# Turned probabilities of the first and the third unit in the places of two late weight blocks, with the order laid out anew, in a block-sparse attention kernel with a channel mixer

## The chip, the cores and the metric

The kernel runs on one core of a Trainium2 chip. The metric is the device time of one launch in microseconds (us), the median over runs. Nothing is shared with other cores. The program is one straight line of instructions for each engine: TensorE (PE, with its weight loads PEld), VectorE (DVE), ScalarE (ACT), GpSimd (POOL), and SyncE (SP), which issues all transfers.

## The reference

Attention with a block mask over 4 batches, 8 heads, 768 tokens and 64 channels, then a gated mixer over the 512 joined channels:

```python
scores = scale * np.matmul(q, k.transpose(0, 1, 3, 2))
mask = np.abs(blk_i - blk_j) <= window
mask = mask | (blk_i == 0) | (blk_j == 0) | (blk_i == n_blocks - 1) | (blk_j == n_blocks - 1)
for qb in range(n_blocks):
    for kb in sampled_blocks[qb]:
        mask[qb * block:(qb + 1) * block, kb * block:(kb + 1) * block] = True
...
attn = attn / (np.sum(attn, axis=-1, keepdims=True) + 1e-09)
attn_out = np.matmul(attn, v).astype(np.float32)
x = np.ascontiguousarray(attn_out.transpose(0, 2, 1, 3)).reshape(B, S, H * D)
...
xk = mu_k * x + (1.0 - mu_k) * x_prev;  xr = mu_r * x + (1.0 - mu_r) * x_prev
k = np.maximum(xk @ w_k, 0.0)
v = k * k @ w_v
r = 1.0 / (1.0 + np.exp(-(xr @ w_r)))
return (r * v).astype(np.float32)
```

A block is 32 tokens, so there are 24 blocks. Three blocks per query block are drawn at random and known only at run time. The three weight matrices arrive with 8 bytes for an element.

## The kernel before

**Units.** The attention is cut into 26 units. Unit u0 holds query block 1 of all four batches, u1 holds block 2, and so on to u21. The last four units are the "wide" ones, with the first and the last block of one batch each. A near unit does, for each half `gi` of the heads: scores on PE into PSUM (tile `s`, L402), the row maximum on DVE (`nm`, L412), four exponentials on ACT (`p`, L423), the probabilities turned, and the product with the values on PE (tile `o`, L436 or L475). Units u0 to u3 turn their probabilities with PE transposes (tile `t`, L371), two groups of four for each half, and each group is then copied from PSUM into the tile `pt` by ACT (L375) or DVE (L376). From u4 on the turning is a DVE transpose and a move by transfers. After the products DVE divides by the row sum (`x`, L556 to L567), and PE turns the result for the mixer (`tx`, L597).

**Loads of a unit.** The keys of a near unit stand in eight of the twelve slots of `KA`, its values in `VA`: the two edge blocks, the three near blocks (a ring of three slots, so that a unit loads one new near block), and the three drawn ones, whose numbers SP reads from the tile `packed`. A new near block goes into the slot whose block the unit before was the last to read, so SP waits for PE before it issues that load: L284 for keys, L297 for values. SP issues everything in order, so whatever is queued behind such a load waits too. The program rotates eight transfer semaphores, so a transfer is issued once the one eight places before it has landed.

**Weights.** 20 blocks w0 to w19 of 128 x 512 are loaded with 8 bytes for an element (L187; w0 to w3 of `w_r`, w4 to w11 of `w_k`, w12 to w19 of `w_v`), and each is brought into a high and a low part by six steps that go to ACT, DVE or POOL (size, tail, sign, join, hi, lo). Each block has a place of its own in the on-chip memory, with its own tag.

**Mixer.** Twelve tiles of 256 tokens: gates `r`, hidden units `h`, values `v`, each product as three terms of high and low parts. The first tile needs units u0 to u3.

**What sets the order.** Every step is recorded in a plan. The list `ORDER` says in which order the steps are written out, for all engines together, and `CHOICE` says which engine takes a step that has several ways. Each engine runs its own steps in that order. The tile `pt` has one buffer: `PT_BUFS` is 1, so the first copy into a unit's `pt` waits until the products of the unit before have read theirs.

Of the kernel before, what the change touches and what calls it, by code (L numbers as in the profile page):

```python
# [19 lines left out]
P = 128  # L20
# [10 lines left out]
QB = 4  # L31
# [64 lines left out]
def block_sparse_attention_channel_mix(  # L96
# [262 lines left out]
    def turned(name):  # L359

        return buf([P, 2, 8, P], F32, "pt", PT_BUFS, f"pt{name}")

    def turn(parts, pt, gi, k, name):
# [5 lines left out]
        def tr():  # L369
# [5 lines left out]
            (ACT, 464, 0, lambda: nc.scalar.copy(pt.ap[:, gi, to], tp.ap[:, 0:many])),  # L375
            (DVE, 600, 0, lambda: nc.vector.tensor_copy(out=pt.ap[:, gi, to], in_=tp.ap[:, 0:many])),  # L376
        ], reads=[(tp,)], writes=[(pt, (gi, k))])
# [5 lines left out]
    def near_unit(at, q, first, o):  # L383
# [6 lines left out]
        for gi in range(2):  # L390
# [39 lines left out]
            def pv(pt=pt, gi=gi):  # L430
                for row in range(2):
                    for a in range(2):
                        i, h = 2 * a + row, 4 * gi + 2 * a + row
                        for g in range(2):
                            for j in range(QB):
                                nc.tensor.matmul(  # L436
                                    o[gi].ap[ROWS[j], i * DV : (i + 1) * DV], pt.ap[:, gi, 4 * row + 2 * a + g, ROWS[j]],
                                    VA.ap[:, c0 + g, j, h * DV : (h + 1) * DV], start=(g == 0), stop=(g == 1), skip_group_check=True)

            plan.add(f"u{name} values", PE, N_PV, pv, reads=[(pt, (gi, 0), (gi, 1))] + [(VA, *PLACE(c0, *range(QB)), *PLACE(c0 + 1, *range(QB)))],  # L440
# [392 lines left out]
X_FROM = 6  # L833
MOVE_FROM = 4
# [160 lines left out]
```

## Time and profile before

| | us |
|---|---|
| median of 3 runs | 515.41 (510.9, 515.41, 519.99) |
| the profiled execution, device time | 516.33 |
| its span (first to last instruction) | 514.6 |
| PE busy | 480.9 (93% of the span) |
| DVE busy | 320.7 (62%) |
| ACT busy | 306.4 (60%) |
| POOL busy | 207.5 (40%) |

A time of the profile is counted from the start of the span. The time around the span is 516.33 - 514.6 = 1.7 us. The profiled execution is 0.9 us above the median. A busy share is an average over the whole program; the stretches differ much, so each stretch is read by itself.

### The profile page before, as it was taken

The numbers are of one execution on the slowest core, as the hardware profiler recorded it, in microseconds if no ns is written. First come the engines' busy times: TensorE is split into PE (matmuls) and PEld (weight loads), VectorE is DVE, ScalarE is ACT, GpSimd is POOL, SyncE is SP. The second block draws the span as 40 slices with busy tenths as digits, with TensorE's granted clock in tenths as the row PEclk, the third lists the DMA queues.
The fourth block names the chain that finished last, engine by engine and source line by source line (L and its number), as shares of the span: only waits on it lengthen the run. The fifth ranks groups of instructions, "written<-read, shape, count | busy, mean of one in ns | idle before, by whom it ended". The sixth has DMA issues, their size and how long they took to land.

```text
span 514.6 us, 18098 instructions
## 1 busy us (share of the span) xinstructions
PE 480.9 (93%) x7384; PEld 399.9 (78%) x7384; DVE 320.7 (62%) x608; ACT 306.4 (60%) x701; POOL 207.5 (40%) x253
## 2 busy tenths in 40 slices
PE   4567899999999998999999999999999999999997
PEld 4254577788788787878778878878778879889896
DVE  3667989786786765775675766664765653334231
ACT  2887988867745646546665846655546574455341
POOL 2435546352610723244442432234543525434531
PEclk9689999999999999999999999999999999999999
DMA  7999999798878889888898888999669653100101
GB/s 265 368 343 379 350 337 310 245 279 249 266 214 252 228 217 270 225 258 236 256 264 240 222 258 265 289 275 340 186 158 309 162 137 85 29 22 20 42 22 41
DMA packets 58052, 114.65 MB, mean 223 GB/s; under 512 B 7665, under 2 KB 20721, under 8 KB 55026
## 3 DMA queue, kind: packets, MB, share of 16 engines
q1 hardware_dynamic: 57970, 113.50, 72.3%
q8 instruction: 58, 0.95, 0.7%
q14 instruction: 24, 0.20, 0.1%
HBM read 77.82 MB, written 6.29 MB: 163 GB/s over the span
## 4 chain that ended last, share of the span: by engine, by line
PE 78%; DMA 8%; SPq 4%; ACT 4%; issue 3%; DVE 2%; POOL 1%; POOLq 0%
PE v L772 22%; PE h_2p L737 7%; PE h_0p L737 6%; PE s L402 6%; PE h_1p L737 6%; PE r_1p L716 6%; PE o L475 6%; PE r_0p L716 6%; PE h_3p L737 6%; DMA VA<-vt 3%; DMA KA<-kt 3%; PE sw L496 2%; PE o L538 2%; ACT p L452 1%; SPq L349 1%
## 5 line engine op out<-in xcount | busy, mean ns | idle before, releaser
L772 PE MATMUL v<-w,k 128*128 128x512 f32 (+1 forms) x600 | 138.9, 385 | 0.0
L772 PEld LDWEIGHTS v<-w,k 128*128 128x128 f32 x600 | 107.9, 188 | 26.7 <-issue 4.6
L402 PE MATMUL s<-KA,q 64*32 64x256 f32 x1408 | 47.6, 391 | 15.7 <-DMA raw<-w_k 10.7
L412 DVE TENSOR_REDUCE nm<-s 128x4 f32<-128x1024 f32 x44 | 53.0, 1215 | 14.3 <-PE s L402 14.0
L452 ACT ACTIVATE p<-s,nm 128x256 f32<-128x256 f32 x144 | 60.6, 479 | 0.6
L455 DVE STREAM_TRANSPOSE r<-p 128x1024 f32<-128x1024 f32 x36 | 43.6, 1229 | 10.9 <-ACT p L452 7.1
L402 PEld LDWEIGHTS s<-KA,q 64*32 64x32 f32 x1408 | 26.2, 109 | 30.2 <-POOL w L246 10.7
L475 PEld LDWEIGHTS o<-VA,pt 128*32 128x32 f32 x2304 | 33.9, 109 | 6.6 <-issue 4.4
L716 PE MATMUL r_0p<-w,xr 128*128 128x512 f32 x144 | 36.8, 400 | 1.3 <-issue 1.3
L475 PE MATMUL o<-VA,pt 128*32 128x65 f32 x2304 | 37.3, 221 | 0.8 <-DMA VA<-vt 0.7
L737 PE MATMUL h_2p<-xk,w 128*128 128x256 f32 x288 | 37.8, 284 | 0.2 <-ACT h_0k L752 0.2
L737 PEld LDWEIGHTS h_0p<-xk,w 128*128 128x128 f32 x288 | 35.6, 189 | 3.0 <-issue 1.6
L737 PE MATMUL h_0p<-xk,w 128*128 128x256 f32 x288 | 37.1, 282 | 0.8 <-issue 0.4
L737 PE MATMUL h_3p<-xk,w 128*128 128x256 f32 x288 | 37.4, 285 | 0.0
L737 PEld LDWEIGHTS h_3p<-xk,w 128*128 128x128 f32 x288 | 35.6, 190 | 2.4 <-issue 1.2
L716 PE MATMUL r_1p<-w,xr 128*128 128x512 f32 x144 | 37.2, 398 | 0.0
L737 PEld LDWEIGHTS h_2p<-xk,w 128*128 128x128 f32 x288 | 35.7, 191 | 1.9 <-issue 0.8
L737 PEld LDWEIGHTS h_1p<-xk,w 128*128 128x128 f32 x288 | 35.3, 189 | 2.3 <-DVE rx L576 1.0
L737 PE MATMUL h_1p<-xk,w 128*128 128x256 f32 x288 | 37.0, 283 | 0.0
L666 ACT ACTIVATE xr_0d<-xt,mk 128x128 f32<-128x128 f32 x48 | 19.3, 403 | 21.9 <-DVE xr_0f L673 15.9
L716 PEld LDWEIGHTS r_0p<-w,xr 128*128 128x128 f32 x144 | 26.2, 188 | 7.7 <-issue 1.8
L716 PEld LDWEIGHTS r_1p<-w,xr 128*128 128x128 f32 x144 | 26.0, 189 | 5.3
(237 smaller groups left out, 818.8 us busy)
## 6 DMA issues: line engine op xcount, KB each, us to landing
VA<-vt SPq DMA_DIRECT2D x92, 260.0 KB, 4.3
KA<-kt SPq DMA_DIRECT2D x89, 256.0 KB, 4.2
pt<-r SPq DMA_DIRECT2D x72, 256.0 KB, 4.9
VA<-vw SPq DMA_DIRECT2D x24, 260.0 KB, 5.5
KA<-kq SPq DMA_DIRECT2D x16, 384.0 KB, 5.0
ptw<-rw SPq DMA_DIRECT2D x32, 192.0 KB, 3.8
out<-z SPq DMA_DIRECT2D x23, 256.0 KB, 3.8
q<-qt SPq DMA_DIRECT2D x22, 256.0 KB, 5.8
```

Source lines behind the costliest of these rows:

```text
L349: nc.sync.dma_start(near_values(chunk, j), vt[bass.ds(sampled_block(n, NRAND + j, nc.sync), 1)].rearrange("o w x -> w (o x)"))
L402: nc.tensor.matmul(s.ap[ROWS[j], row, a * 256 : (a + 1) * 256].rearrange("p (n x) -> p n x", x=BLK), q.ap[half, (hp * QB + j) * BLK : (hp ...
L412: nc.vector.tensor_reduce(out=nm.ap.rearrange("p (r a) -> p r a", r=2), in_=s.ap.rearrange("p r (a x) -> p r a x", a=2), axis=AX.X, op=ALU ...
L452: plan.add(f"u{name} exp {i}", ACT, 365, lambda row=row, a=a, i=i: nc.scalar.activation(squares()[:, :, :, i, :], s.ap[:, row, a * 256 : ( ...
L455: plan.add(f"u{name} turn", DVE, N_TURN, lambda: nc.vector.transpose(out=r.ap[:, :, gi].rearrange("p j c i x -> p j (c i x)"), in_=squares ...
L475: nc.tensor.matmul(o[gi].ap[ROWS[j], i * DV : (i + 1) * DV], pt.ap[:, j, gi, g, 2 * row + a, :], VA.ap[:, c0 + g, j, h * DV : (h + 1) * DV ...
L496: nc.tensor.matmul(s.ap[HALF[a], row, 0:W], q.ap[half, 2 * hp * BLK : 2 * (hp + 1) * BLK], wide_keys(b, hp)[half, k * W : (k + 1) * W], st ...
L538: nc.tensor.matmul(o.ap[ROWS[2 * a + e], c * DV : (c + 1) * DV], pt.ap[:, 2 * a + e, row, n, :], VA.ap[:, c1, part, h * DV : (h + 1) * DV] ...
L666: nc.scalar.activation(parts(d.ap), cols(c, 0), AF.Copy, scale=mk.ap[:, which, c : c + 1])
L716: nc.tensor.matmul(pr.ap[:, 0:512], xr.ap[:, a, c, :], weight_of["r", c].ap[:, w, :], start=(c == 0 and m == 0), stop=(c == CC - 1 and m = ...
L737: nc.tensor.matmul(ph.ap[:, ff * TT : (ff + 1) * TT], weight_of["k", c, f2 // 2].ap[:, w, f % 4 * P : (f % 4 + 1) * P], xk.ap[:, a, c, :], ...
L772: nc.tensor.matmul(pv.ap[:, 0:width], k2.ap[:, a, f, i * P : (i + 1) * P], weight_of["v", f].ap[:, w, cs], start=(f == 0 and m == 0), stop ...
```

## The change

For u0 and u2 the tile of turned probabilities is no longer the one buffer `pt`. Each half goes into the place of a weight block, half 0 into that of w18 and half 1 into that of w19. Those two weight blocks can then be loaded only once u2's products have read their probabilities. u1 and u3 keep the one buffer `pt`. The table `ORDER` is new for the first 584 of its 2139 steps (to about the scores of u8) and the same from there on. Some 80 entries of `CHOICE` differ, all of steps in that first part; the warm-up on PE goes from 128 small matmuls to 1.

```diff
-    def turned(name):
-
-        return buf([P, 2, 8, P], F32, "pt", PT_BUFS, f"pt{name}")
+    def turned(at):
+
+        if at in GUESTS:
+            halves = [buf([P, 8, P], F32, f"w{w}", 1, f"pt{at}_{w}") for w in GUESTS[at]]
+            return halves, lambda gi: halves[gi].ap
+        one = buf([P, 2, 8, P], F32, "pt", PT_BUFS, f"pt{at}")
+        return [one, one], lambda gi: one.ap[:, gi]
...
-            (ACT, 464, 0, lambda: nc.scalar.copy(pt.ap[:, gi, to], tp.ap[:, 0:many])),
-            (DVE, 600, 0, lambda: nc.vector.tensor_copy(out=pt.ap[:, gi, to], in_=tp.ap[:, 0:many])),
-        ], reads=[(tp,)], writes=[(pt, (gi, k))])
+            (ACT, 464, 0, lambda: nc.scalar.copy(pt[1](gi)[:, to], tp.ap[:, 0:many])),
+            (DVE, 600, 0, lambda: nc.vector.tensor_copy(out=pt[1](gi)[:, to], in_=tp.ap[:, 0:many])),
+        ], reads=[(tp,)], writes=[(pt[0][gi], (gi, k))])
...
-                                    o[gi].ap[ROWS[j], i * DV : (i + 1) * DV], pt.ap[:, gi, 4 * row + 2 * a + g, ROWS[j]],
+                                    o[gi].ap[ROWS[j], i * DV : (i + 1) * DV], pt[1](gi)[:, 4 * row + 2 * a + g, ROWS[j]],
...
 X_FROM = 6
+GUESTS = {0: (18, 19), 2: (18, 19)}
 MOVE_FROM = 4
...
 CHOICE = {
-    "warm": 6, "u0 1 1 turned": 1, "u0 put x": 1, "u1 1 0 turned": 1, "u2 0 0 turned": 1, "u3 0 0 turned": 1, "u3 1 0 turned": 1, "u4 put x": 1, "u5 put x": 1, "u6 put x": 1,
+    "warm": 2, "u0 0 1 turned": 1, "u0 1 0 turned": 1, "u0 1 1 turned": 1, "u1 0 0 turned": 1, "u1 0 1 turned": 1, "u1 1 1 turned": 1, "u2 0 1 turned": 1, "u2 1 0 turned": 1,
...
 ORDER = [
-    0, 1, 2, 7, 16, 3, 11, 994, 973, 924, 14, 931, 4, 5, 13, 12, 10, 15, 926, 927, 925, 55, 966, 928, 933, 934, 56, 932, 974, 935, 996, 936, 6, 8, 995, 18, 937, 929, 997, 53,
+    2, 1, 3, 14, 16, 973, 55, 10, 917, 4, 5, 11, 931, 12, 7, 9, 974, 975, 13, 976, 15, 977, 932, 17, 934, 978, 979, 933, 935, 19, 918, 936, 920, 994, 6, 56, 0, 980, 53, 34,
```

**SP, the start of the program.** `raw` is a weight block, `KA` keys, `q` the queries, and the row on `packed` stands right ahead of u0's three drawn key loads. Before:

```order
L159 DMA mk<-mu_r 128x4
L137 DMA drawn<-blocks 1x1848
L284 DMA KA<-kt 128x512
L187 DMA raw_210<-w_k 128x1024
L187 DMA raw_212<-w_k 128x1024
L187 DMA raw_214<-w_r 128x1024
L284 DMA KA<-kt 128x512
L187 DMA raw_217<-w_r 128x1024
L159 DMA mk<-mu_k 128x4
L284 DMA KA<-kt 128x2x512
L305 DMA q_233<-qt 128x512
L266 TENSOR_LOAD packed
```

and with the change:

```order
L137 DMA drawn<-blocks 1x1848
L284 DMA KA<-kt 128x512
L187 DMA raw_78<-w_k 128x1024
L305 DMA q_81<-qt 128x512
L187 DMA raw_83<-w_r 128x1024
L159 DMA mk<-mu_k 128x4
L284 DMA KA<-kt 128x512
L187 DMA raw_98<-w_r 128x1024
L284 DMA KA<-kt 128x2x512
L159 DMA mk<-mu_r 128x4
L266 TENSOR_LOAD packed
```

Three weight blocks instead of four stand ahead of u0's drawn keys, and the drawn block numbers are the first transfer.

**SP, from the load that waits for u0's scores to the last load of u0's values.** `L284 DMA KA` is the near key block of u1, which waits for u0's scores; `L349` are the drawn values of u0, `L297` near or edge values. Before:

```order
L284 DMA KA<-kt 128x512
L187 DMA raw_346<-w_r 128x1024
L187 DMA raw_354<-w_k 128x1024
...
L349 DMA VA<-vt 32x2080
...
L297 DMA VA<-vt 32x2080 x2
L266 TENSOR_LOAD packed
```

and with the change:

```order
L284 DMA KA<-kt 128x512
L187 DMA raw_213<-w_v 128x1024
L297 DMA VA<-vt 32x2080
...
L349 DMA VA<-vt 32x2080
...
L297 DMA VA<-vt 32x2080
L305 DMA q_270<-qt 128x512
L266 TENSOR_LOAD packed
```

Two of u0's near and edge value blocks have gone ahead (they now stand right behind u0's drawn keys), and one weight block instead of two stands between.

**PE, from the end of the warm-up to u0's products.** `s` are scores, `t0` the turns of u0, `o` the products; `pt_371` is the one buffer, `pt_19` and `pt_18` are the new places. Before:

```order
L171 MATMUL warm<-const-bfloat16-1.0 128x64
L402 MATMUL s_1_291<-KA,q_233 32x256 x16
L402 MATMUL s_0_315<-KA,q_233 32x256 x16
...
L371 MATMUL t0 0 0_443<-ident,p_0_362 128x128 x4
L436 MATMUL o_1_472<-VA,pt_371 32x65 x32
L436 MATMUL o_0_511<-VA,pt_371 32x65 x32
L371 MATMUL t1 1 1_557<-ident,p_1_464 128x128 x4
L371 MATMUL t1 1 0_571<-ident,p_1_464 128x128 x4
```

and with the change:

```order
L171 MATMUL warm<-const-bfloat16-1.0 128x64
L406 MATMUL s_1_163<-KA,q_81 32x256 x16
L406 MATMUL s_0_183<-KA,q_81 32x256 x16
...
L375 MATMUL t0 0 0_308<-ident,p_0_224 128x128 x4
L440 MATMUL o_1_328<-VA,pt_19_230 32x65 x32
L440 MATMUL o_0_368<-VA,pt_18_322 32x65 x32
L375 MATMUL t1 1 1_419<-ident,p_1_316 128x128 x4
L375 MATMUL t1 1 0_430<-ident,p_1_316 128x128 x4
```

But for the warm-up the order of PE is the same here: the turns of u1 still stand behind the products of u0. So it is at the two later seams: the turns of u2 stand behind the products of u1, and those of u3 behind the products of u2, before and now.

## Rows read from the trace of the kernel before

**Rows 1.** Page, part 2: busy tenths in 40 slices of 12.9 us.

```profile
PE   4567899999999998999999999999999999999997
```

**Rows 2.** Stretches: PE, PEld, DVE, ACT, POOL busy; granted clock; transfer share; GB/s.

```profile
15.00:30.00 15.00, 8.53 (x144) 4.55 (x144) 11.79 (x16) 12.72 (x28) 6.81 (x6) 0.78 0.98 365
30.00:45.00 15.00, 10.92 (x326) 8.61 (x327) 10.13 (x20) 12.77 (x29) 5.13 (x5) 0.89 0.99 361
45.00:60.00 15.00, 11.56 (x294) 8.24 (x301) 12.23 (x32) 12.36 (x34) 8.57 (x11) 1.00 0.96 357
75.00:90.00 15.00, 14.26 (x266) 12.44 (x265) 14.45 (x28) 12.53 (x27) 8.01 (x9) 1.00 0.94 316
200.00:300.00 100.00, 97.98 (x1584) 82.12 (x1584) 66.55 (x130) 63.55 (x150) 42.34 (x53) 1.00 0.86 247
```

**Rows 3.** Timeline of PE: start, length, tiles, count, idle before and its releaser.

```profile
0.77 5.81 PE L171 MATMUL warm<-const-bfloat16-1.0 128*128 128x64 bf16 x128 [0.77 <-PEq L943]
17.23 3.67 PE L402 MATMUL s<-KA,q 64*32 64x256 f32 x64 [10.65 <-DMA raw<-w_k]
31.89 3.65 PE L436 MATMUL o<-VA,pt 128*32 128x65 f32 x128 [4.06 <-DMA VA<-vt]
46.45 0.43 PE L436 MATMUL o<-VA,pt 128*32 128x65 f32 x14 [2.62 <-issue]
46.81 0.66 PE L371 MATMUL t2 0 0_757<-ident,p 128*128 128x128 f32 x4
57.98 1.09 PE L402 MATMUL s<-KA,q 64*32 64x256 f32 x32
60.62 1.12 PE L436 MATMUL o<-VA,pt 128*32 128x65 f32 x64
66.68 2.67 PE L402 MATMUL s<-KA,q 64*32 64x256 f32 x64 [0.82 <-DMA KA<-kt]
69.28 0.96 PE L716 MATMUL r_0p<-w,xr 128*128 128x512 f32 x3
```

**Rows 4.** Chain that ended last, 25 to 67 us: start, length, what.

```profile
25.46 6.30 DMA VA<-vt
35.39 6.62 DMA VA<-vt
60.79 5.76 DMA KA<-kt
```

**Rows 5.** Timeline of SP's issues: start, length, line, tile.

```profile
17.00 0.50 SPq L297 DMA_DIRECT2D VA<-vt  x1
21.02 0.34 SPq L284 DMA_DIRECT2D KA<-kt  x1
43.72 0.57 SPq L187 DMA_DIRECT2D raw<-w_k  x1
46.91 0.50 SPq L297 DMA_DIRECT2D VA<-vt  x1
```

**Rows 6.** Stretches of 2 us, columns as in rows 2.

```profile
8.00:10.00 2.00, 0.00 (x0) 0.00 (x0) 0.00 (x0) 0.00 (x0) 0.00 (x0) 1.00 1.03 406
12.00:14.00 2.00, 0.00 (x0) 0.00 (x0) 0.69 (x1) 1.44 (x3) 0.98 (x2) 0.50 1.06 396
```

**Rows 7.** Transfers issued from 0 to 90 us: count, KB each, median us to landing.

```profile
KA<-kt SPq DMA_DIRECT2D x32, 256.0 KB, 5.0
VA<-vt SPq DMA_DIRECT2D x28, 260.0 KB, 5.9
raw<-w_k SPq DMA_DIRECT2D x8, 512.0 KB, 5.6
q<-qt SPq DMA_DIRECT2D x8, 256.0 KB, 5.9
```

**Rows 8.** Page, part 3: the instructions' own queue: packets, MB, share.

```profile
q8 instruction: 58, 0.95, 0.7%
```

**Rows 9.** Groups of DVE, 0 to 70 us: count, busy us, mean ns, idle before.

```profile
L376 DVE COPY pt<-t0 1 1_366 128x512 f32<-128x512 f32 x1 | 0.7, 692 | 0.8 <-PE t0 1 1_366 L371 0.8
```

More of the change, by code (lines that the diff above doesn't have):

```diff
@@ L436, in pv @@
                                 nc.tensor.matmul(
-                                    o[gi].ap[ROWS[j], i * DV : (i + 1) * DV], pt.ap[:, gi, 4 * row + 2 * a + g, ROWS[j]],
+                                    o[gi].ap[ROWS[j], i * DV : (i + 1) * DV], pt[1](gi)[:, 4 * row + 2 * a + g, ROWS[j]],
                                     VA.ap[:, c0 + g, j, h * DV : (h + 1) * DV], start=(g == 0), stop=(g == 1), skip_group_check=True)
-            plan.add(f"u{name} values", PE, N_PV, pv, reads=[(pt, (gi, 0), (gi, 1))] + [(VA, *PLACE(c0, *range(QB)), *PLACE(c0 + 1, *range(QB)))],
+            plan.add(f"u{name} values", PE, N_PV, pv, reads=[(pt[0][gi], (gi, 0), (gi, 1))] + [(VA, *PLACE(c0, *range(QB)), *PLACE(c0 + 1, *range(QB)))],
                      writes=[(o[gi], 0)], table="values", code=128)
```

181 rows, old and new, of tables (CHOICE, ORDER) are left out of this document.

## The prediction

> **What bounds the kernel now.** I read the page first, for the slices of PE [rows 1]. PE is at nine tenths or more from the sixth slice on, but for one eight and the last slice; what it loses lies in the first five, some 64 us. The stretches say it in numbers [rows 2]: from 15 to 60 us PE is busy 8.5 to 11.6 of every 15 us while the transfer share is 0.96 to 0.99; from 75 to 90 us PE is at 14.26, and from 200 to 300 us at 97.98 of 100. So a gain or loss of the first 70 us is carried to the end almost whole, and nothing behind it can be won by this change, since the order there is the same.
>
> Then I read PE's timeline for what it waits on [rows 3]. It waits 10.65 us for u0's keys, 4.06 us for u0's values, 2.62 us in the middle of u1's products with no semaphore behind it ("issue"), and 0.82 us for u5's keys. The chain of waits has the landings [rows 4]: u0's last value block at 25.46 + 6.30 = 31.76, u1's at 35.39 + 6.62 = 42.01, u5's keys at 60.79 + 5.76 = 66.55. Last I read SP's own timeline [rows 5]: between 17.50 and 21.02 it waits for u0's scores, since u1's near key block goes into a slot that they read, and between 44.29 and 46.91 for the end of u1's products, for u2's near value block.
>
> **The stream of loads.** With 256 KB for a key block or a unit's queries, 260 KB for a value block and 512 KB for a weight block [rows 7], I count along SP's order what has to be loaded up to a given load:
>
> | up to and with | before, KB | now, KB |
> |---|---|---|
> | u0's drawn keys | 4096 | 3584 |
> | u0's last value block | 9244 | 8220 |
> | u1's last value block | 12848 | 12848 |
> | u2's last value block | 16192 | 16192 |
> | u4's keys | 17984 | 18240 |
> | u3's last value block | 19024 | 20048 |
> | u5's keys | 21328 | 21328 |
>
> From u0's last value to u5's keys the stream carried 21328 - 9244 = 12084 KB in 66.55 - 31.76 = 34.8 us [rows 4], 347 KB/us. Its best stretch had 406 GB/s, 396 KB/us [rows 6].
>
> **The change, part by part.**
>
> *The guest places.* By themselves I cost them at nothing. They free u1's copies from waiting for u0's products, and u3's from u2's. But PE has the turns of u1 behind the products of u0 and those of u3 behind the products of u2, before and now, so there was no such wait to remove. The cost would be the loads of w18 and w19, which must wait for u2's products; w18 stands right behind a value block of u3 that waits for the same products, so it adds no wait.
>
> *The start.* One weight block less is ahead of u0's drawn keys: 512 / 396 = 1.3 us. The first scores go from 17.23 to 15.9.
>
> *The warm-up.* 5.81 us of PE go, inside an idle stretch that ends with the keys: no gain. Nor a loss: the granted clock is back at 0.50 of full speed from 12 to 14 us [rows 6], five us before the first scores, which run at that level (3.67 us for 64) [rows 3].
>
> *u0's values.* From 17.2, where the first scores start [rows 3], to 31.76 the stream carried 9244 - 4096 = 5148 KB, 354 KB/us with SP's wait of 3.5 us in it, which stays (u1's key block still stands behind u0's scores). Now 8220 - 3584 = 4636 KB are left: 13.1 us, landing at 29.0 instead of 31.76. PE is 2.8 us ahead here.
>
> *u1's values.* Both orders need 12848 KB. From 29.0 that is 4628 KB more at 352 (the rate between the first two landings of rows 4): 42.1 against 42.01. **The lead is given back**; PE now waits here instead.
>
> *The gap of 2.62 us in u1's products.* Before, PE entered these products without a pause and ran dry of instructions. Now it has u0's products, the turns and the scores of u2 behind it by about 37 and waits some 5 us for values, time in which instructions can come. I take the gap as gone: u1's products end 2.6 us earlier, at 44.3.
>
> *What follows.* u2's near value block is issued when these products end, so 2.6 us earlier, and the stream behind it moves with it. u5's keys: 21328 - 16192 = 5136 KB at 347 is 14.8 us behind u2's last value (46.91 [rows 5] and about 5 to land [rows 7] before, 49.2 now), so 64.0 instead of 66.55. But u3's last value now has 1024 KB more ahead of it: 49.2 + 3856 / 347 = 60.3, where PE had u3's products at 60.62. From there PE still has u3's two halves of products (1.12 each), a turn (0.66) and three pieces of the first gate (0.96 each) [rows 3]: 5.8, or about 5.5 since neighbours overlap a little; then u5's scores, 2 x 1.09: 60.3 + 5.5 + 2.2 = 68.0. Before, the same work was done at 69.28 + 0.96 = 70.24. **Gain 2.2 us.**
>
> *The other engines.* Up to u4's maxima DVE gets six copies of turned probabilities more, 6 x 0.69 = 4.1 us [rows 9], and about half of it back in weight steps that go elsewhere. DVE stood idle 4.9 us from 30 to 45 and 2.8 us from 45 to 60 [rows 2], which covers that and an advance of 2.2 us, but not much more; from 75 to 90 it has 0.6 us left. ACT gets six copies fewer.
>
> **Sum.** Span 514.6 - 2.2 = 512.4, with the 1.7 around it 514.1 for an execution like the profiled one. That one is 0.9 above the median of its kernel, so the median goes from 515.41 to **513.2 us**. The bounds of the unknown parts: nothing at all if the gap stays or is paid as another wait; 6.0 us if the stream ran all the way at its best rate (15.9 + 17744 / 396 = 60.7 for u5's keys instead of 66.55).
>
> **Two rules weighed.** The row of the instructions' own queue has 58 packets for 0.95 MB [rows 8], and the gap of 2.62 us has no other releaser. The Trainium skill, "Runtime: NRT & Kernel Launch", Instruction fetch mechanics, has instructions come in blocks of 16 KiB, 256 instructions, fetched while the block before runs, and calls the cost of a boundary mostly hidden. The packets agree with the block size; the gap does not agree with "hidden". By the page the gap should not come back; by the row, which shows it on a PE that ran without pause, it may, wherever PE catches up, and then the sum is 0 instead of 2.2.
>
> An idle PE loses its clock here: after 4.06 us of idle u0's products took 3.65 us for 128, against 1.12 us for 64 later on [rows 3]. The Trainium skill, "TensorE: Matmul & The Clock Gate", What's actually happening, calls the low level the default that activity releases. That speaks against this change, and it is the third rival.
>
> **The rivals.**
>
> 1. *Nothing is won*, 0.20: the gap returns elsewhere, or the loads of u2 come no sooner. For it: equal KB in the table at u1, u2 and u5. Against it: SP's wait for u1's products is real. 515.4 us.
> 2. *The stream gets faster*, 0.13: weight blocks spread between small loads keep it near 396 KB/us. For it: 406 GB/s in some stretches. Against it: 316 to 365 GB/s as a mean, with both of SP's long waits kept. 6.0 us: 509.4 us.
> 3. *The clock drops in the new wait ahead of u1's products*, 0.12: they then take 3.65 instead of 2.1 us, 1.5 us more, of 2.2 us gained 0.7 is left: 514.7 us.
> 4. *Slower, by u3's values*, 0.14: they stand 1024 KB later, 2.95 us at 347. It decides if the stream behind u2's values is not at least 1.2 us earlier than before; with no advance at all they land 2.95 us behind 60.6, PE ends u5's scores at 63.5 + 5.5 + 2.2 = 71.2, 1 us late, and where PE's order gives no work to fill in, up to 2.95 late. I take 2: 517.4 us.
>
> **How the numbers follow.** My forecast has 0.37; the remaining 0.04 are for something larger than any of these. The likeliest time is 513.2 us. The runs of the kernel before lie 4.5 us to either side of their median, so a median of a few runs may be 2 to 3 us off by itself. The range takes in rivals 2 and 4 with some of that: 507.5 to 518.5 us. 2% is 10.3 us, about what a measurement of this kernel can tell from no change; no case above reaches that, the best by the loads alone is 6.0. With the scatter: faster 0.05, within 0.90, slower 0.05.
>
> **What the profile after would show.** First scores of u0 near 15.9, at half clock; u0's products near 29; an idle stretch of PE ahead of u1's products of some 5 us with values as releaser, and u1's products near 42; no gap of 2.6 us inside them; u2's near value block issued near 44.3; u5's scores done near 68; from there on the busy shares of before. I would be wrong if u1's products began well before 41, for then the stream was faster than counted, or if PE waited on DVE or ACT between 45 and 65, for then the copies moved to DVE are not covered.

## The result, and the profile after

The changed kernel took 519.52 us (median of 22 runs, 516.35 to 526.46), the kernel before beside it 517.5 us (22 runs): ratio 1.006, 95% interval 1.0036 to 1.0083. By the ratio it is slower by 3.1 us (1.9 to 4.3), where 2.2 us less were forecast. The profiled execution has a span of 518.5 us and took 520.29 us. The ratios here leave out the executions that took over 1.5% longer than the fastest of their kernel, and the traces of e3 and e13 are of such executions.

Stretches of the kernel after, columns as in [rows 2]:

```profile
0.00:15.00 15.00, 1.59 (x33) 0.99 (x41) 5.53 (x14) 6.40 (x10) 5.47 (x11) 1.00 0.84 313
15.00:30.00 15.00, 10.30 (x264) 6.31 (x248) 11.12 (x19) 11.63 (x28) 6.50 (x7) 1.00 0.99 361
30.00:45.00 15.00, 8.25 (x164) 5.52 (x168) 9.07 (x15) 8.71 (x20) 8.30 (x8) 0.77 1.00 370
45.00:60.00 15.00, 10.79 (x293) 7.88 (x293) 11.88 (x31) 10.82 (x28) 9.33 (x10) 0.96 0.78 265
0.00:75.00 75.00, 45.22 (x1004) 30.07 (x1005) 50.48 (x95) 48.99 (x111) 35.86 (x43) 0.93 0.92 330
```

The first and the last of these for the kernel before:

```profile
0.00:15.00 15.00, 5.81 (x128) 5.72 (x128) 4.82 (x13) 4.61 (x7) 4.45 (x10) 0.88 0.84 283
0.00:75.00 75.00, 50.37 (x1154) 37.73 (x1155) 52.58 (x101) 55.73 (x128) 33.65 (x42) 0.91 0.95 340
```

Up to 45 us the changed kernel has moved more: 313, 361 and 370 GB/s against 283, 365 and 361, together 0.53 MB ahead. From 45 to 60 us it moves 265 GB/s against 357, 1.38 MB less, and at 75 us it is 0.75 MB behind (330 against 340 GB/s).

PE's timeline of the kernel after, columns as in [rows 3]; the last row is a block of 128 products that both kernels have in the same place of their order:

```profile
13.62 3.67 PE L406 MATMUL s<-KA,q 64*32 64x256 f32 x64 [12.64 <-DMA KA<-kt]
26.43 2.15 PE L440 MATMUL o<-VA,pt 128*32 128x65 f32 x128 [2.47 <-DMA VA<-vt]
32.99 0.66 PE L375 MATMUL t1 0 1_445<-ident,p 128*128 128x128 f32 x4 [3.22 <-ACT p L427]
34.75 3.63 PE L406 MATMUL s<-KA,q 64*32 64x256 f32 x64 [1.10 <-DMA KA<-kt]
41.62 1.12 PE L375 MATMUL t1 0 0_541<-ident,p 128*128 128x128 f32 x4 [2.65 <-ACT pt L379]
42.66 3.00 PE L440 MATMUL o<-VA,pt 128*32 128x65 f32 x114
47.37 0.43 PE L440 MATMUL o<-VA,pt 128*32 128x65 f32 x14 [1.70 <-issue]
56.48 0.66 PE L375 MATMUL t3 0 0_847<-ident,p 128*128 128x128 f32 x4 [1.41 <-ACT p L427]
59.16 2.17 PE L406 MATMUL s<-KA,q 64*32 64x256 f32 x32 [0.36 <-issue]
65.01 1.01 PE L440 MATMUL o<-VA,pt 128*32 128x65 f32 x56 [0.54 <-DMA VA<-vt]
72.19 1.09 PE L406 MATMUL s<-KA,q 64*32 64x256 f32 x32
93.29 2.03 PE L479 MATMUL o<-VA,pt 128*32 128x65 f32 x128
```

The same block in the kernel before:

```profile
90.61 2.03 PE L475 MATMUL o<-VA,pt 128*32 128x65 f32 x128
```

The reader sees a start that is 3.6 us early (13.62 against 17.23 [rows 3]), u0's products 5.5 us early (26.43 against 31.89), and then two waits for ACT and one for keys, until u1's products end at 47.80, 0.9 us later than before (46.88). Behind them PE waits 1.41 us for u3's exponentials on ACT (before, it waits 1.68 us for a copy on ACT near there), and u4's first scores take 2.17 us for 32 products, where they took 1.09 [rows 3]. At 90 us PE is 2.68 us late (93.29 against 90.61), of 3.9 us between the two spans.

SP's timeline of the kernel after, as in [rows 5]:

```profile
41.96 0.57 SPq L187 DMA_DIRECT2D raw<-w_k  x1
47.84 0.49 SPq L297 DMA_DIRECT2D VA<-vt  x1
51.55 0.33 SPq L284 DMA_DIRECT2D KA<-kt  x1
53.21 1.70 SPq L332 DMA_DIRECT2D KA<-kt  x3
60.40 0.53 SPq L297 DMA_DIRECT2D VA<-vt  x1
```

And three shorter stretches of it, columns as in [rows 2]:

```profile
42.00:46.00 4.00, 3.66 (x118) 3.17 (x117) 1.32 (x3) 4.00 (x12) 2.34 (x2) 0.62 1.02 393
46.00:48.00 2.00, 0.63 (x16) 0.54 (x16) 0.16 (x1) 0.49 (x2) 1.72 (x2) 1.00 0.46 170
60.00:62.00 2.00, 2.00 (x29) 1.11 (x13) 1.65 (x4) 1.60 (x4) 1.38 (x3) 0.50 0.92 306
```

SP comes to u2's near value block at 42.53 and stands until u1's products are done, 47.84: 5.3 us, before 2.6 [rows 5]. Transfers issued earlier keep the engines full until some 46.5, four microseconds into the stand; then they run dry. Before, the stand began at 44.29 and was over within 2.6 us, and the share from 46 to 48 us was 0.92. From 60 to 62 us the granted clock is 0.50 of full speed, where u4's first scores (59.16 to 61.33) took twice as long as before.

ACT's timeline of the kernel after shows what PE waited for (columns as for PE):

```profile
31.29 0.67 ACT L201 ACTIVATE wmag<-raw 128x512 f32<-128x512 f32 x1 [2.08 <-DMA raw<-w_r]
33.84 0.67 ACT L201 ACTIVATE wmag<-raw 128x512 f32<-128x512 f32 x1 [0.90 <-DMA raw<-w_k]
37.34 0.68 ACT L201 ACTIVATE wmag<-raw 128x512 f32<-128x512 f32 x1 [2.84 <-DMA raw<-w_r]
39.76 0.20 ACT L420 ACTIVATE nm<-nm 128x4 f32<-128x4 f32 x1 [1.23 <-DVE nm L416]
41.00 0.56 ACT L379 COPY pt<-t1 1 0_430 128x512 f32<-128x512 f32 x1
```

ACT stands three times for a weight block that is still loading, 5.8 us in all, with u1's exponentials and its second copy queued behind. The copy has one more thing ahead of it: ACT's share of u2's row maximum (`nm`), for which ACT waits 1.23 us. The chain that ended last (columns as in [rows 4]) goes that way: from u2's keys, which stand behind two weight loads on SP, over u2's scores and DVE's maximum to the copy. So PE's wait of 3.22 us goes back to the weight blocks, and that of 2.65 us, in this chain, to u2's keys. The last row is the landing of u3's last values:

```profile
26.95 7.75 DMA KA<-kt
34.75 3.73 PE s L406 x64
38.50 1.24 DVE nm L416
41.14 0.44 ACT pt L379
60.40 4.57 DMA VA<-vt
```

### The profile page after: what moved, and what is told of

It reads as the page before. It is cut to its first block, busy times and chain, and to the rows that moved or that the text cites. A ratio compares the mean times of both kernels' runs of the same rounds, so it can differ in the third digit from the quotient of the medians.

```text
span 518.5 us, 17843 instructions
## 1 busy us (share of the span) xinstructions
PE 477.6 (92%) x7257; PEld 395.1 (76%) x7257; DVE 321.9 (62%) x612; ACT 303.7 (59%) x694; POOL 208.4 (40%) x251
## 4 chain that ended last, share of the span: by engine, by line
PE 65%; SPq 14%; DMA 9%; DVE 4%; issue 4%; ACT 3%; POOL 0%; ACTq 0%
PE v L776 16%; PE h_2p L741 6%; PE r_1p L720 6%; PE s L406 6%; PE h_1p L741 5%; PE h_3p L741 5%; PE h_0p L741 5%; PE r_0p L720 5%; SPq L467 4%; PE o L479 4%; DMA KA<-kt 3%; SPq L349 2%; PE o L542 2%; PE sw L500 2%; SPq L332 2%
## 5 line engine op out<-in xcount | busy, mean ns | idle before, releaser
L406 PE MATMUL s<-KA,q 64*32 64x256 f32 x1408 | 49.1, 408 | 17.5 <-DMA KA<-kt 15.1
L456 ACT ACTIVATE p<-s,nm 128x256 f32<-128x256 f32 x144 | 60.7, 479 | 2.1 <-PE t3 1 1_1017 L375 1.5
L406 PEld LDWEIGHTS s<-KA,q 64*32 64x32 f32 x1408 | 27.4, 112 | 31.9 <-issue 22.9
L420 ACT ACTIVATE nm<-nm 128x4 f32<-128x4 f32 x44 | 8.8, 202 | 38.4 <-DVE nm L416 38.4
```

What stands on the lines that cost most here:

```text
L406: nc.tensor.matmul(s.ap[ROWS[j], row, a * 256 : (a + 1) * 256].rearrange("p (n x) -> p n x", x=BLK), q.ap[half, (hp * QB + j) * BLK : (hp ...
L456: plan.add(f"u{name} exp {i}", ACT, 365, lambda row=row, a=a, i=i: nc.scalar.activation(squares()[:, :, :, i, :], s.ap[:, row, a * 256 : ( ...
```

## The experiments

Every kernel of an experiment was run in five rounds beside the kernel before, 6 to 12 times in all, and the kernel after 22 times. "Landmark" is the start of the block of 128 products that begins at 90.61 in the kernel before; "0 to 75" is the mean GB/s of that stretch, and with the share of 45 to 60 us it comes from the same view as the stretches above. Both are of one profiled execution each. In the edits below + is the place where a step is put and - the place where it stood.

| kernel | ratio, 95% interval | 0 to 75 | share 45 to 60 | landmark |
|---|---|---|---|---|
| before | 1 | 340 | 0.96 | 90.61 |
| after | 1.0060, 1.0036 to 1.0083 | 330 | 0.78 | 93.29 |
| e1 no guests | 1.0044, 1.0006 to 1.0081 | 329 | 0.86 | 93.66 |
| e2 guests only | 1.0007, 0.9973 to 1.0040 | 341 | 0.98 | 90.50 |
| e3 ACT first | 1.0069, 1.0026 to 1.0112 | 322 | 0.75 | 95.42 |
| e4 SP: u2's and u4's keys | 1.0001, 0.9958 to 1.0043 | 336 | 0.96 | 91.69 |
| e5 u4's keys only | 1.0047, 1.0015 to 1.0079 | 330 | 0.97 | 92.85 |
| e6 u2's keys only | 1.0016, 0.9978 to 1.0053 | 324 | 0.74 | 95.56 |
| e7 before, u4 late | 1.0021, 0.9991 to 1.0051 | 339 | 0.96 | 91.36 |
| e8 e3 and e4 | 1.0093, 1.0061 to 1.0124 | 331 | 0.89 | 92.91 |
| e9 e8, 107 warm-ups | 1.0024, 0.9980 to 1.0069 | 334 | 0.98 | 92.01 |
| e10 after, filled stand | 1.0046, 1.0001 to 1.0090 | 335 | 0.93 | 91.39 |
| e11 before, 107 warm-ups | 0.9981, 0.9946 to 1.0016 | 346 | 0.99 | 89.79 |
| e12 e9 and e10 | 1.0007, 0.9975 to 1.0039 | 333 | 0.97 | 91.89 |
| e13 before, loads behind | 1.0037, 1.0005 to 1.0069 | 327 | 0.76 | 94.88 |
| e14 e11 and a filled stand | 1.0001, 0.9965 to 1.0036 | 340 | 0.96 | 89.87 |
| e15 before, 1 warm-up | 0.9975, 0.9943 to 1.0006 | 339 | 0.91 | 90.61 |
| e16 before, 90 warm-ups | 1.0063, 1.0027 to 1.0100 | 337 | 0.96 | 89.79 |

Over these 18 traces the landmark follows the bytes moved by 75 us: the correlation is -0.95, and 1 GB/s less over 75 us (75 KB) puts the landmark back by 0.28 us. That is a link between two rows of the same execution; which of the two leads is what e10 and e13 were made for, and neither settles it. With the ratios the landmark goes together much less (0.49), and the share of 45 to 60 us no better (-0.42): a ratio is a mean over 6 to 22 executions, which lie some 4 us to either side of their median, and a trace is one of them. From the landmark to the end the traced executions differ as well, by 5.5 us (423.9 us in e10, 429.4 us in e3), with almost the same work left to do.

**e1 and e2: the places or the order?**

```
e1, in the kernel after:  GUESTS = {0: (18, 19), 2: (18, 19)}  ->  GUESTS = {}
e2, in the kernel before: the new turned() with GUESTS, and the old ORDER and CHOICE
```

> The changed kernel with its order and its choices of engines, but u0 and u2 turn their probabilities into the one buffer again. If the guest places move nothing (the turns of u1 and u3 stand on PE behind the products that free the buffer): 1.006 of the kernel before, as the change itself, within 0.3%, and u1's products end near 47.8 us as in the change. If waiting for the two weight places is what costs: near 1.000. If the guest places give part of a gain that the order then loses: slower than the change, 1.010 or more.

> The kernel before with its own order and choices, but u0 and u2 turn into the places of w18 and w19. If the guest places move nothing: 1.000 within 0.3%, and PE's waits up to 70 us as before (10.7, 4.1, 2.6 us). If they help by themselves: 0.995 or less. If they cost, since two weight loads now wait for u2's products: 1.004 or more.

Without guests the loss stays (1.0044, from 1.0006), and guests alone make none that can be told (1.0007, up to 1.0040). In e1's trace u1's products end at 46.24 and not near the 47.8 that was expected. What follows is about the order, with the choices of engines that go with it.

**e3 and e4: ACT's order or SP's?**

```
e3, ACT: + u1 0 exp 2, + u1 1 0 turned, w1 size, ... - u1 0 exp 2, ... - u1 1 0 turned
e4, SP:  + u2 keys 5, w1 load, w7 load, - u2 keys 5
         + u4 drawn keys, u4 keys 4, + u5 q, - u5 q, - u4 drawn keys
```

> The changed kernel with two steps moved on ACT: u1's last exponential and u1's copy of the second turned group go ahead of the size and sign steps of the weight blocks w1, w7 and w3, which wait for loads. Theory of blocked queues: PE's wait of 3.2 us ahead of u1's third turn goes, its wait of 2.65 us ahead of the fourth shrinks to under 1 us, u1's products end 1 to 3 us earlier than 47.8, SP's wait of 5.3 us for them shrinks by the same, and the time goes to 1.000 to 1.004. Theory of bytes (u3's values stand 1024 KB later, nothing else): 1.006 as the change.

> The changed kernel with SP's order mended in two places: u2's near key block ahead of the two weight blocks w1 and w7, and u4's drawn keys ahead of u4's near key block, which waits for u3's scores (and u5's queries behind it). Theory of blocked queues: u2's scores start about 2.5 us earlier than 34.75, SP's wait of 1.2 us at u4's near keys no longer holds up three drawn keys, u4's scores end near 61 instead of 63.3, time 1.000 to 1.004. Theory of bytes (u3's values later): 1.006, since u3's values keep their place.

PE's timeline of e3:

```profile
30.48 0.63 PE L375 MATMUL t1 0 1_446<-ident,p 128*128 128x128 f32 x4 [0.44 <-DVE pt L380]
35.95 3.67 PE L406 MATMUL s<-KA,q 64*32 64x256 f32 x64 [4.84 <-DMA KA<-kt]
47.78 0.66 PE L440 MATMUL o<-VA,pt 128*32 128x65 f32 x14 [2.86 <-issue]
```

The waits for ACT are gone (3.22 to 0.44) and nothing is won: PE waits 4.84 us for u2's keys instead. So ACT was not the only thing late; but this trace is of the slowest of e3's twelve executions. The ratio of 1.0069 misses the 1.000 to 1.004 of the theory. e4 has the time of the kernel before (1.0001), with a share of 0.96 from 45 to 60 us. Its interval and that of the change overlap, so a recovery is not proved; and in its trace u2's scores begin at 35.82, 1.1 us later than 34.75, where 2.5 us earlier were expected.

**e5, e6, e7: which of e4's two moves?**

```
e5, SP of the kernel after:  + u4 drawn keys, u4 keys 4, + u5 q, - u5 q, - u4 drawn keys
e6, SP of the kernel after:  + u2 keys 5, w1 load, w7 load, - u2 keys 5
e7, SP of the kernel before: - u4 drawn keys, u4 keys 4, + u5 q, + u4 drawn keys
```

> The changed kernel with one move on SP: the three drawn key blocks of u4 stand ahead of u4's near key block and u5's queries behind it, as in the kernel before; u2's keys stay behind the loads of w1 and w7. Theory A (the loss is made at 50 us: SP waits there for u3's scores with four loads behind it): the share of the DMA engines from 45 to 60 us returns from 0.78 to 0.9 or more, u4's scores start at 58 to 58.5 instead of 59.2, the ratio to the kernel before is 0.998 to 1.002. Rival B (it is made at 35 us, by u2's keys behind two weight loads): ratio 1.004 to 1.008, as the changed kernel, share of 45 to 60 us below 0.85.

> The changed kernel with the other move on SP alone: u2's near key block ahead of the loads of w1 and w7. Theory A: ratio 1.004 to 1.008, since SP still stands at u4's near keys with u4's drawn keys behind it, and u1's products end at 46.5 to 47.8 as before. Rival B: u2's scores begin below 34, u1's products end before 46, and the ratio is 0.998 to 1.002.

> The kernel before with the disputed step of the change alone, put in: u4's near key block, then u5's queries, then u4's three drawn key blocks on SP (before: drawn, then near). Theory A: slower, ratio 1.002 to 1.006, with u4's scores 0.5 to 1.5 us behind 57.98 and the share of 45 to 60 us below 0.92. Rival B: no change, ratio 0.998 to 1.002.

Theory A of e5 fell: the share of 45 to 60 us did return to 0.97, and the time did not (1.0047, landmark 92.85); the bytes were lost from 30 to 45 and from 60 to 75 us instead (330 GB/s over 75). Rival B has the ratio right and the share wrong. Nor did e7 lose its share (0.96) or clearly its time. e6's ratio is the better of the two, but in its trace the loss is as large as in any (324 GB/s, landmark 95.56). No single place of SP's order is shown to be the cause.

**e8 and e9: both moves, and the instructions.**

```
e8: the kernel after with the moves of e3 and e4
e9: e8, and  WARM: (1, 64, 60)  ->  (107, 64, 60)
```

> The changed kernel with both SP moves and with u1's last exponentials and its second transposed copy ahead of w1's work on ACT. Theory C (the ACT wait and the keys of u2 cover each other in this stretch, either alone leaves the other): u1's products begin below 41 and end before 45.5, SP's wait for them ends before 45.5, the ratio is 0.994 to 0.999, and it could beat the kernel before by 1 to 2 us. Rival D (the transfers set the pace from 45 to 65 us, share 0.95 or more, whatever PE has in hand at 45): PE's lead is turned into waits for transfers by 65 us and the ratio is 0.999 to 1.003.

> Both SP moves and both ACT moves of e8, and 107 warm-up products of 64 columns in place of 1, so that the places in PE's instruction stream where the traces show an issue wait (every 256 instructions: 962 in the changed kernel and in e8, the 114th of the 128 matrix products of u1's values) come 106 products earlier: the 8th of u1's products, and the next one behind their end. Theory E (in e8 u1's products stood complete but for 14 from 44.36 to 46.65 because their instructions came late, and that held SP's load of u2's near values): no issue gap inside u1's products, they end at 44 to 45.3, the near value block is issued below 45.5, 45 to 60 us moves 5.1 MB or more (4.63 in e8), the offset to the kernel before at 90 us is below 1.2 us (2.29 in e8), ratio 0.996 to 1.002. Rival F (the ACT moves themselves cost, or the wait only moves to u3's scores): ratio 1.005 or more, offset at 90 us above 2.

PE's timeline of e8:

```profile
40.80 1.66 PE L440 MATMUL o<-VA,pt 128*32 128x65 f32 x64 [3.94 <-DMA VA<-vt]
42.63 1.72 PE L440 MATMUL o<-VA,pt 128*32 128x65 f32 x50 [0.17 <-DVE pt L380]
46.65 0.43 PE L440 MATMUL o<-VA,pt 128*32 128x65 f32 x14 [2.29 <-issue]
```

And of e9:

```profile
42.15 3.78 PE L440 MATMUL o<-VA,pt 128*32 128x65 f32 x128 [4.41 <-DMA VA<-vt]
48.32 0.27 PE L375 MATMUL t2 0 1_761<-ident,p 128*128 128x128 f32 x1 [1.31 <-issue]
```

In e8 u1's products begin at 40.80, the earliest of all, wait for values as I had forecast, and then stand at the 114th product for an issue wait that ends at 46.65. The ratio, 1.0093, is the worst of all and outside both expectations, while the traced execution, 517.62 us, is the fastest of e8's six: the trace doesn't show what the others lost. With 106 more instructions of each kind ahead (e9), that wait comes behind the products, as theory E has it, and the share of 45 to 60 us is 0.98 in place of 0.89. e9's end of the products, 45.93, missed the 44 to 45.3 that was expected: they began later and took 3.78 us, as at half clock. The landmark, 1.40 late, missed too (below 1.2). Ratio 1.0024 against 1.0093, intervals that overlap by a hair.

**e10 and e12: fill the stand.**

```
e10, SP of the kernel after: w5 load, + u4 q, + w6 load, u2 values 1 1, - u4 q, - w6 load
e12: e9 with the same move
```

> The changed kernel with u4's queries and the load of w6 (768 KB) ahead of u2's near value block on SP, so that SP has something to issue before it stands for u1's products. Theory A' (the loss is the bytes that are not moved while SP stands): the DMA share from 45 to 60 us rises from 0.78 to 0.88 or more, 20.1 MB or more are moved by 60 us (19.64 in the changed kernel, 20.49 in the kernel before), the offset at 90 us falls from 2.7 to 0.5 to 1.5, ratio 0.998 to 1.003. Rival G (PE's own waits for ACT and DVE in u1 and u2 are the loss): offset at 90 us 2 or more, ratio 1.004 to 1.008.

> All moves together: e9 and the two loads of e10 ahead of u2's near values. Theory A' with E: by 45 us 15.5 MB or more (15.13 in the kernel before), by 60 us 20.6 or more, the offset at 90 us 0 to -1.5 us, ratio 0.995 to 1.000. Rival F: as in e9, ratio 1.005 or more; rival H (from 60 us on PE is the bound whatever the transfers do): by 60 us the bytes are ahead of the kernel before and the offset at 90 us is 0 to 1 all the same.

PE's timeline of e10:

```profile
42.76 2.03 PE L440 MATMUL o<-VA,pt 128*32 128x65 f32 x128
```

Its stretch of 45 to 60 us:

```profile
45.00:60.00 15.00, 11.40 (x255) 8.04 (x254) 13.16 (x31) 11.56 (x30) 9.13 (x11) 0.89 0.93 318
```

In this trace the stand is almost gone (SP issues the near value block at 45.40), the share is back, and the landmark is 0.78 late, as theory A' expects. But its products also ran without an issue wait and at full speed, 2.03 us, which the move doesn't explain, and the ratio says 1.0046: the profiled execution is the fastest of its twelve. By the ratio A' was missed, though its interval reaches down to 1.0001. e12 came out level with the kernel before (1.0007); its landmark, 1.28 late, missed the lead that was expected.

What the move doesn't explain is a difference between executions. The kernel after, e1, e5 and e10 have the same order on every engine up to the last load ahead of u2's near values, 42 to 44 us on SP; e1 lacks the guest places besides. Their traces are four draws of one start. u1's products in e1, then in e5:

```profile
42.54 3.70 PE L440 MATMUL o<-VA,pt 128*32 128x65 f32 x128
44.08 2.93 PE L440 MATMUL o<-VA,pt 128*32 128x65 f32 x128
```

With 42.66 in the kernel after and 42.76 in e10 they begin within 1.6 us of each other, behind a wait of 2.2 to 2.7 us for the copy on ACT each time. They end at 47.80, 46.24, 47.01 and 44.79: the gap came in one of four, half speed in three. The kernel before draws as well: in e2 and e7, which have its order up to there, the gap of 2.62 us is 1.35 and 1.23 us. And e1, e5 and e10, without a gap in their traces, have ratios of 1.0044 to 1.0047. So the gap is not shown to be what makes the loss.

**e11, e14, e15, e16: the kernel before with parts of the change.**

```
e11: WARM[6] (128, 64, 60) -> (107, 64, 60)
e14: e11, and on SP  + w4 load, u2 values 1 1, - w4 load
e15: CHOICE "warm": 6 -> 2, that is 1 product
e16: WARM[6] (128, 64, 60) -> (90, 64, 60)
```

> The kernel before with 107 warm-up products in place of 128, nothing else: the issue wait of 2.62 us inside u1's products (instruction 1218) comes to stand behind them, at u2's transposes. Theory E: no issue gap inside u1's products, they end near 44.3 in place of 46.88, SP issues u2's near value block at once when it comes to it (44.3 in place of 46.91). What that is worth is small, since the DMA engines were busy to 0.96 from 45 to 60 us: 0 to 0.6 us, ratio 0.998 to 1.001. Rival (the wait is tied to the place in the work, not to the count): the gap stands at the 114th product as before.

> The kernel before with 107 warm-up products (as e11) and with the load of w4 (512 KB) ahead of u2's near value block, so that SP has one more load to issue before it would stand. Theory A' with E: the wait before the near value block is below 1 us (2.6 in the kernel before, 1.4 in e11), 25.5 MB or more by 75 us, offset at 90 us 0 to -1.5 us, ratio 0.995 to 0.999. Rival H (e11's gain was chance): offset 0 to +0.5, ratio 0.999 to 1.002.

> The kernel before with 1 warm-up product in place of 128, nothing else: the warm-up part of the change alone. My prediction's step (the removed warm-up costs nothing and, with SP's order as before, gains nothing): the first scores start at 16.5 to 17.3 (17.23 before), the offset at 90 us is within 0.7 us, ratio 0.998 to 1.002. Rival: with the warm-up gone PE's first instruction block is loaded out of the way and the first scores start 0.5 us or more sooner; or PE's lower clock at the first scores costs 1 us or more at 90 us.

> The kernel before with 90 warm-up products in place of 128, nothing else. By e15 and e11: the early instruction packet of 9 us isn't there, so that SP's third drawn key block is issued a microsecond sooner and the first scores start at 16.0 to 16.4 (17.23 before); and the issue wait of instruction 962 comes at the 25th of u1's products, and the next one behind them, so that u1's products end at 43.5 to 45.5 in place of 46.88. Theory A' with E: 25.6 MB or more by 75 us, offset at 90 us -0.5 to -1.5 us, ratio 0.994 to 0.999, and it may be the first kernel here that is faster than the kernel before. Rival H (neither e11 nor e15 is more than chance): ratio 0.999 to 1.003, offset at 90 us -0.3 to +0.7.

PE's timeline of e11:

```profile
42.19 3.39 PE L436 MATMUL o<-VA,pt 128*32 128x65 f32 x120 [0.33 <-DMA VA<-vt]
```

Of e15:

```profile
16.17 3.67 PE L402 MATMUL s<-KA,q 64*32 64x256 f32 x64 [15.20 <-DMA raw<-w_k]
```

Of e16:

```profile
94.17 0.66 PE L475 MATMUL o<-VA,pt 128*32 128x65 f32 x30 [2.14 <-issue]
335.02 0.30 PE L475 MATMUL o<-VA,pt 128*32 128x65 f32 x2 [2.25 <-issue]
```

e11 has no issue wait in u1's products; together with e9 this speaks for a wait that goes by the count of instructions and not by the place in the work, as does the count in the last section. They ended at 45.58 all the same, not near 44.3: 120 of them took 3.39 us, as at half speed. e15 has the first scores at 16.17 in place of 17.23, as its rival had it. Both look faster by 0.2%, which their intervals do not tell from no change. e16 was to have both, has both in its trace (first scores at 16.11, no gap, landmark 0.8 early), and is slower, 1.0063: of three cuts of the warm-up alone two made no difference that can be told and one cost 3 us. In its trace the loss comes after 90 us, in issue waits of 2.14 and 2.25 us in products; the longest of the kernel before behind 90 us is 0.81. That is outside both expectations. e14, with nothing left of the stand (44.77 to 44.87), has the time of the kernel before (0.995 to 0.999 was expected): taking the 2.6 us stand away won nothing that can be told. No version beat the kernel before by more than its interval.

**e13: a stand put into the kernel before.**

```
e13, SP: - w15 load, u2 drawn values, - w9 load, u2 values 1 1, + w9 load, + w15 load
```

> The kernel before with the loads of w15 and w9 (1024 KB) behind u2's near value block on SP instead of ahead of it; PE, ACT and DVE keep their order. SP then comes to that block some 2 to 2.8 us sooner and stands longer for u1's products. Theory A' (the loss is the bytes not moved while SP stands): the wait before the near value block grows from 2.6 us to 4 us or more, the bytes moved by 60 us fall from 20.49 to 20.0 MB or less, the offset to the kernel before at 90 us is +1 to +2.5 us, ratio 1.002 to 1.005. Rival G (the loss of the change lies in the orders of ACT, DVE and PE): offset below 0.7 us, ratio 0.998 to 1.001.

PE's, then ACT's timeline of e13:

```profile
54.16 1.11 PE L371 MATMUL t2 1 0_869<-ident,p 128*128 128x128 f32 x4 [3.77 <-ACT xt L618]
```

```profile
52.88 0.66 ACT L201 ACTIVATE wmag<-raw 128x512 f32<-128x512 f32 x1 [4.86 <-DMA raw<-w_v]
```

Its stretch of 45 to 60 us:

```profile
45.00:60.00 15.00, 10.51 (x234) 7.96 (x233) 8.87 (x24) 8.00 (x23) 6.18 (x8) 0.77 0.76 279
```

The loss is there (1.0037, 1.0005 to 1.0069), with PE, ACT and DVE in their old orders: two weight loads moved behind a value block on SP are enough. But the stand that I named grew only to 2.8 us; the one that cost came later. ACT stood 4.86 us for the late weight block, PE 3.77 us for ACT, and SP 4.0 us (54.70 to 58.74) for PE, at u3's near values. Its profiled execution, 523.64 us, is the slowest of its twelve, so the landmark exaggerates, and the way that the loss takes in this trace need not be that of the others.

## Why the prediction was wrong

- **The guest places cost and win nothing**: nothing in e1 and e2 speaks against it (no difference over 0.4%).
- **The start, 1.3 us**: 3.61 us. The term was mis-sized twice. SP's order goes with about 2.5 (from 0 to 15 us 313 GB/s were moved in place of 283), by difference; and the warm-up, which I had at nothing, held the first scores back by 1.06 (e15). It is not its 5.81 us of work: with 90 products (e16) they start at 16.11, with 107 (e11) at 17.00. The kernels with 107 or 128 have an instruction packet at about 9 us, e15 and e16 have none before 20 us; how it would hold the keys back is not shown.
- **u0's values at 29.0**: u0's products began at 26.43, 2.6 us sooner, nearly all of it from the start (13.62 in place of 15.9).
- **The lead given back at u1's values, 42.1**: u1's products began at 42.66, for another reason. PE waited for ACT's copy (2.65), behind u2's keys, scores and maximum; the values were there, and in e8, which waits for them, they came at 40.80.
- **The gap gone, u1's products ending at 44.3**: this is the step that failed, and with it the advance of 2.6 us on which the whole gain rests. They ended at 47.80: 0.56 for the later start, 1.2 because they ran at half speed for most of their length (3.00 and 0.43 us against 2.2), and 1.70 for the gap, which came back at the same product. I had reasoned that PE's wait ahead would give the instructions time to come. The wait was there, and in e1, e4, e5 and e10 the gap was away; here and in e3, e6 and e8 it was not. It differs between executions of one order, and the sum took it as settled. In the other three traces of this order the products ended at 44.8 to 47.0: what failed in all four is 44.3, by 0.5 to 3.5 us.
- **u2's near value block 2.6 us earlier**: 0.93 us later (47.84); in e1 and e5, the same order, 46.29 and 47.08, so 0.6 us earlier and 0.2 us later. So the stream was not released, it was stopped for 5.3 us, and the 0.53 MB won up to 45 us became 0.75 MB lost by 75 us.
- **u3's last value at 60.3, u5's scores done at 68.0**: PE had u3's values at 65.01 and u5's scores done at 73.28; 0.9 us of it are six products of the first hidden tile between the halves of u5's scores, which the sum left out. Rival 4 had named this end: it was to decide if the stream behind u2's values wasn't at least 1.2 us earlier. It was later, and the chain ends a landing of u3's values at 64.97. Its price, 2 us, lies in the measured 1.9 to 4.3, but that is luck in good part: PE itself waited 0.54 us for these values (2.28 in e1, 0.15 in e10, not at all in e5).
- **Rival 3, the clock**: it was one part of it, 0.62 of 2.4 GHz granted as the mean from 42 to 46 us, behind 2.65 us of idle PE. It came again at u4's scores, 1.08 us more at 0.50 from 60 to 62 us, which no rival had.
- **The other engines**: I counted how much ACT and DVE had to do and not behind what it was queued. ACT got five copies fewer in all (11 before, 6 now) and became what PE waited on: 3.22 us behind weight blocks not yet loaded, 2.65 us behind u2's maximum. My sign for being wrong, a wait on ACT or DVE between 45 and 65, did come (1.41 us at 56.48, 0.57 at 58.14), though the kernel before has 1.68 us for ACT there too; the two longest waits lie ahead of that stretch.
- **The median**: 519.52 lies above the range to 518.5, and 6.3 us above 513.2. Of these 2.1 are the kernel before's own (517.5 in these runs, 515.41 in those shown ahead), 2.2 the gain that didn't come, and 2.0 the loss between the two medians, which the ratio puts at 3.1.
- **Small things in the sums**: rows 7 give a value block 5.9 us to land, not 5, which makes the gain 1.3 in place of 2.2; the best case is 66.55 - 60.7 = 5.85, not 6.0; and 406 GB/s is not the best stretch of the kernel before, which has 415 from 42 to 44 us.

What is shown: the loss is there with the order and the choices and without the places (e1), and can't be told with the places alone (e2); and moving two loads on SP is enough for a loss of this kind (e13). In the traced execution of the kernel after, 2.7 of 3.9 us lie ahead of the landmark, and they go with the 1.38 MB that are not moved from 45 to 60 us. That such missing transfers are the cause of the mean loss is argued, not shown: e5, e8 and e10 have shares of 0.89 to 0.97 there and ratios of 1.0046 to 1.0093, and e6 has 0.74 and 1.0016. Nor is it shown which move of the order is to blame. Each wait that was taken away (ACT's in e3, both in e8) let the next one decide: u2's keys, u1's values, the instructions. And the time of e16, and of e8 and e10 against their traces, stays open; some 0.5% goes with where waits and transfers fall in an execution, which one trace of a kernel doesn't tell.

## What to carry to other kernels

Where one queue issues all loads in order, follow what it stands for: a load that waits for a buffer stops every load behind it, and a lead won earlier only brings the queue to that stand sooner. Work out first how long the loads already issued last (here some 4 us, 42.53 to 46.5), since a shorter stand did not empty the transfer engines here (2.6 us: a share of 0.96 from 45 to 60 us). For an engine with an order of its own, read behind what its next step is queued, not only how busy it is. And a trace is one execution: before a wait in it is blamed, look whether it is there in the trace of another kernel with the same order up to that place.

## What the runs showed of the hardware

All issue waits of 0.6 us or more in the 18 traces stand a multiple of 256 instructions of PE apart, to within two, if products, weight loads and the semaphore instructions between them are counted together: at the 962nd here and in e8, at the 1218th in the kernel before, in e9 and in e14. The instruction queue has about one 16 KB packet for each such step: 57 for 14,668 instructions of PE here, 58 for 14,928 before [rows 8]. From 44 to 47 us, the kernel after (queue, kind, packets, MB, share):

```profile
q8 instruction: 1, 0.02, 2.0%
```

From 38.6 to 41 us, e4:

```profile
q8 instruction: 1, 0.02, 3.2%
```

By the same count PE came to the 706th instruction, where the block before begins, at about 38 us in both. The packet starts at 39.7 in e4, and there is no gap; here it starts at 45.2, and PE goes on at 47.37. In e1, e5 and e10, the same order up to there, it starts between 39.5 and 40.3. What holds it back in the one execution is not shown. The Trainium skill, "Runtime: NRT & Kernel Launch", Instruction fetch mechanics, calls the crossing mostly hidden: no gap at most crossings agrees; 1.70, 2.29 and 2.86 us at the same one (here, in e8 and in e3), with a transfer share of 0.94 to 1.02 from 42 to 46 us, do not.

At the start the granted clock is printed as 1.00 from 0 to 30 us, yet the 64 scores from 13.62 on took 3.67 us, as long as at 0.50 in the kernel before (17 to 21 us) [rows 3], and e15's did too, at 16.17. There the duration of the products speaks for half speed, and the printed figure does not.
